# Start of a fused FFT and gated feed-forward kernel on one core: batch 0 loaded with a cast and folded by TensorE, its shuffle through DRAM in blocks, weights on the GpSimd queue

## The chip, the cores and the metric

The kernel runs on one core of a Trainium2 chip. The metric is the device time of one execution in microseconds. Three runs of the kernel before gave 648.35, 649.7 and 650.36 us (median 649.7). A further execution was profiled; its own time is given with the profile.

## The reference: what is computed

The input `x` has the shape (8, 3008, 256). A two-dimensional Fourier transform is taken over sequence and feature dimension, and its real part goes through a gated feed-forward layer: two projections, the first cut at zero, are multiplied and projected back:

```
X   = fft(fft(x, axis=1), axis=2).real            # (8, 3008, 256)
tok = X.reshape(24064, 256)
out = (max(tok @ w_gate, 0) * (tok @ w_val)) @ w_out   # w_gate, w_val: 256 x 1536, w_out: 1536 x 256
```

All inputs and the output are float32. The kernel computes products in bfloat16.

## The kernel before

**The transform.** 3008 is split as 94 x 32 (`NA`, `NB`). Since x is real, the transform has a mirror symmetry, and the kernel uses it twice: rows r and S - r are formed from the same two products (the "direct" and the "mirrored" half of each output block), and the input is *folded* first: row j is added to its mirror row, and columns d and 256 - d are added and subtracted. `fold` (line 96) does this for batches 1 to 7 on GpSimd, from four tiles (`xla`, `xlb` low half of the rows, `xha`, `xhb` mirrored rows), in 23 pieces per batch; the mirrored rows come by an indirect load (line 92) that walks the partitions backwards. Batch 0 has a path of its own: `load_first` (line 123) brings eight plain pieces on SP's queue, `fold_first` (line 131) folds columns only, on VectorE and GpSimd, and stage 1 adds the mirrored rows with a second set of tables, `w1h`.

**Stages of the transform.** `stage1` (line 170) multiplies by the 94-point tables (`w1`, and `wz` for the two end rows), two rows per call, and copies the result to the tile `t1`. `shuffle_out` (line 199) writes `t1` to a DRAM buffer `Td`, and `shuffle_in` (line 204) reads it back with partition and free index exchanged, as the tile `t4` with 12 slabs, four for each of the three blocks (`NBLK`) of a batch. `rotate` (line 210) repairs one column of `t4` by a small product. `stage2` (line 218) makes the 32-point transform of a block in two halves (`cs` 0 and 1), writes the block `pq`, and after half 1 sends row 0 of it through DRAM to get it on all partitions (`nb`, lines 236 and 237).

**The weights.** The transform over the feature dimension is multiplied into the weights. `load_w` loads three column groups n = 0, 1, 2 (called W0, W1, W2; `i` 0 is gate, 1 is value), `pair_w` (line 272) adds and subtracts their halves, `fold_w` (line 278) multiplies them with a cosine or sine table `cd` in float32 and writes `wc`, `ws`, and `wm` (scaled `ws`).

**The layer.** A step t is one batch, block and slice of 128 of the 1536 hidden columns: 8 x 3 x 12 = 288 steps. `gate` and `mirror_gate` make G (lines 517, 518, 524), `value` makes V (line 532), VectorE and ACT combine them, `mirror_h` (line 552) multiplies the mirrored half on GpSimd, except in the first block, where VectorE does it; `out_piece` (line 581) multiplies by `w_out`, and `store` (line 632) writes rows to DRAM. Steps 0 to 11 are the first block and run without the output products; from step 12 on two steps form a pair, and the output products of 12 steps earlier run between.

**What sets the order.** All engines run in the order of the program, written out by hand. The dictionary `extra`, filled by `at(t, ...)` (line 640 on), places transforms, weight folds and loads of later batches behind single steps; `plan` gives the steps of stage 1, shuffle, rotation and stage 2 for the next batch. `pace` hands GpSimd the pieces of `fold`, so many per step. A one-element copy to `seen` on GpSimd (line 457) waits for the shuffled batch 0; the indirect loads of batch 1, the load of `wo`, `pair_w` of W2 and the fold of batch 1 stand behind it on that engine. SP issues its transfers in program order too: x of batch 0, W0, half of W1, the shuffle, the rest of W1, W2, x of batch 1.

**At the end**, the last output block is copied out in four pieces (line 586); nothing is stored after the first, the first two together after the second, and the others by one, over SP's and ACT's queues.

**Warm products.** 32 products of a zero tile (`WARM`, line 338) run on TensorE ahead of all.

Of the kernel before, what the change touches and what calls it, by code (L numbers as in the profile page):

```python
# [19 lines left out]
WARM = 32  # L20
# [23 lines left out]
def kernel(ctx: ExitStack, tc, x, w_gate, w_val, w_out, out):  # L44
# [51 lines left out]
    def fold(b, eng):  # L96


        eo = xt[b]["eo"] = tp.tile([NA, J, D], BF16, tag="eo", name="eo")
        for half, chunks in enumerate(((1, 3, 5, 7), (9, 11, 13))):  # L100
# [16 lines left out]
            if 1 < b < B - 1:  # L117
                load_x(b + 1, half, nc.sync)


    FIRST = (0, 28, 4, 24, 8, 20, 12, 16)

    def load_first():
        t = {0: x_tile(True, 0), 1: x_tile(True, 1), 2: x_tile(False, 1), 3: x_tile(False, 0)}
        for r in FIRST:
            nc.sync.dma_start(out=t[r // JH][:, r % JH:r % JH + 4, :],
                              in_=view(x, r * D, [[NB * D, 96], [1, 4 * D]]))
        t["e"] = [tp.tile([NA, J, D], BF16, tag="eo", name="eo") for i in range(2)]
        xt[0] = t

    def fold_first(r, n, op, eng):

        t, e = xt[0][r // JH][0:NA], xt[0]["e"][r // 16]
        lo = r % 16

        def part(a, n, o, op, swap):
            p0 = free(t, (a % JH) * D + 1, [D, n], [1, H - 1])
            p1 = free(t, (a % JH) * D + D - 1, [D, n], [-1, H - 1])
            eng.tensor_tensor(e[:, a:a + n, o:o + H - 1], p1 if swap else p0, p0 if swap else p1, op=op)  # L139

        if op == ALU.add:
            part(lo, n, 1, ALU.add, False)
            eng.tensor_copy(free(e[:], lo * D, [D, n], [H, 2]), free(t, (lo % JH) * D, [D, n], [H, 2]))
        elif r == 16:
            part(0, 1, H + 1, ALU.subtract, False)
            part(1, n - 1, H + 1, ALU.subtract, True)
        else:
            part(lo, n, H + 1, ALU.subtract, r > 16)
# [12 lines left out]
    def early(name):  # L161

        if turn["v"] % 2 == 0:
            turn["t"] = psv.tile([128, 2, 512], F32, tag="v", name=name)
        turn["v"] += 1
        return turn["t"][:, (turn["v"] - 1) % 2, :]
# [3 lines left out]
    def stage1(b, c, evac):  # L170
        if b not in t1t:
            t1t[b] = tp.tile([96, 16, D], BF16, tag="t1", bufs=1, name="t1")
        t1 = t1t[b]
        eo, eh = xt[b]["e"] if b == 0 else (xt[b]["eo"], None)
        ps = early("ps1") if b == 0 else borrow("ps1")
        for i in range(2):
            jj = 2 * c + i
            o = ps[0:96, i * D:(i + 1) * D]
            if jj and b == 0:
                nc.tensor.matmul(o, lhsT=w1[:, jj, :], rhs=eo[:, jj, :], start=True, stop=False)  # L180
                nc.tensor.matmul(o, lhsT=w1h[:, NB // 2 - jj, :], rhs=eh[:, NB // 2 - jj, :], start=False, stop=True)  # L181
            elif jj:
                nc.tensor.matmul(o, lhsT=w1[:, jj, :], rhs=eo[:, jj, :], start=True, stop=True)  # L183
            else:
                ends = (eo[:, 0, :], eh[:, 0, :] if b == 0 else eo[:, J - 1, :])
                for cs, lo, hi in ((0, 0, H + 1), (1, H + 1, D)):
                    for k in range(2):
                        nc.tensor.matmul(ps[0:96, lo:hi], lhsT=wz[:, cs, k, :], rhs=ends[k][:, lo:hi],
                                         start=(k == 0), stop=(k == 1))
        dst = free(t1[:], 2 * c * D, [H, 4], [H // 2, 2], [1, H // 2])  # L190
# [5 lines left out]

    t4t = {}

    def shuffle_out(b, c0, c1):
# [103 lines left out]
    with tc.tile_pool(name="sp", bufs=1, space=SB) as sp:  # L303
# [159 lines left out]
        for _ in fold(1, pl):  # L463
            pass
# [291 lines left out]
```

## Time and profile before

| what | value |
|---|---|
| runs shown | 648.35, 649.7, 650.36 us |
| profiled execution, its own time | 646.91 us |
| its span, first to last instruction | 645.1 us |
| mean granted TensorE clock | 0.987 |
| busy share: TensorE, VectorE, ACT, GpSimd | 96%, 85%, 69%, 81% |
| start to the first gate product | 36.42 us |
| first block (steps 0 to 11) | 36.42 to 64.03 us |
| steps 12 to 287 | 64.03 to 627.42 us |
| output products of the last block | 627.42 to 637.93 us |
| from there to the end of the span | 7.17 us |

Rows of a timeline read: start, duration, engine, line, operation, output <- inputs, partitions x elements, count, and in brackets the idle time before with what ended it. PE is TensorE's product, PEld its weight load, DVE VectorE, POOL GpSimd, SPq, ACTq and POOLq the engines' issue of transfers. Product records overlap: the time one takes in a row of products is read from the distance of the starts.

### The profile page before, as it was taken

The page shows a single profiled execution, that of the slowest core. Times are in us where ns is not written, and L with a number is a line of the kernel's source. Part 1 is how long each engine was busy: PE and PEld are TensorE (multiplying, and loading weights), DVE is VectorE, ACT ScalarE, POOL GpSimd, SP SyncE. Part 2 cuts the span into 40 slices and gives each one's busy share as a digit, 9 for nine tenths or more (in the row PEclk, how much of TensorE's full clock was granted, in tenths as well). Part 3 has the DMA queues.
Part 4 walks back from the last instruction along what each step waited for, and adds up shares of the span by engine and source line. Part 5 has one row for each costly group of instructions (what it writes and reads, how often), then busy time and mean ns, then how long its engine had stood idle before and what let it go on. Part 6 is the DMA issues. An engine that isn't in the chain of part 4 may idle for free.

```text
span 645.1 us, 11866 instructions
## 1 busy us (share of the span) xinstructions
PE 618.7 (96%) x4231; PEld 410.4 (64%) x4231; DVE 549.3 (85%) x642; ACT 444.7 (69%) x846; POOL 521.9 (81%) x436
## 2 busy tenths in 40 slices
PE   6878999899999999999999999999999999999995
PEld 3423666666666666666666666676666666666664
DVE  9847888788988988988988897888988898899991
ACT  5455687667677767677777776777677777766660
POOL 9559989999999999999998999898555555556661
PEclk9699999999999999999999999999999999999999
DMA  9694753562735284344723555211512133212114
GB/s 248 197 242 68 173 147 83 153 161 67 207 83 137 43 234 103 106 102 114 195 65 87 121 142 150 59 33 37 156 51 60 46 93 93 67 33 65 32 39 92
DMA packets 35635, 70.72 MB, mean 110 GB/s; under 512 B 6124, under 2 KB 23508, under 8 KB 32244
## 3 DMA queue, kind: packets, MB, share of 16 engines
q1 hardware_dynamic: 32152, 57.92, 34.2%
q0 software_dynamic: 3120, 11.80, 8.0%
q8 instruction: 33, 0.54, 0.4%
q10 hardware_dynamic: 304, 0.25, 0.2%
q14 instruction: 26, 0.21, 0.1%
HBM read 39.77 MB, written 30.96 MB: 110 GB/s over the span
## 4 chain that ended last, share of the span: by engine, by line
PE 82%; DMA 5%; POOL 5%; DVE 3%; ACT 2%; issue 1%; SPq 1%; ACTq 0%; POOLq 0%; DVEq 0%
PE po L581 35%; PE V L532 17%; PE G L524 8%; PE G L518 8%; PE G L517 8%; DMA t<-Td 2%; DMA Td<-t 2%; PE ps L183 2%; POOL eo L139 2%; PE ps L225 1%; PE psw L282 1%; DVE E L539 1%; POOL h L552 1%; SPq L632 1%; DVE h L545 1%
## 5 line engine op out<-in xcount | busy, mean ns | idle before, releaser
L552 POOL TENSOR_TENSOR h<-gm,E 128x992 bf16<-128x992 f32 (+1 forms) x138 | 319.9, 2318 | 87.2 <-DVE E L559 51.7
L581 PE MATMUL po<-wo,h 128*128 128x256 bf16 (+2 forms) x2304 | 326.0, 272 | 0.0
L581 PEld LDWEIGHTS <-h 128*128 128x128 bf16 (+2 forms) x2304 | 231.7, 103 | 106.1
L526 ACT ACTIVATE gm<-G 128x496 f32<-128x496 f32 (+1 forms) x288 | 170.3, 591 | 101.0 <-PE G L524 95.9
L545 DVE TENSOR_TENSOR h<-gs,V 128x1024 bf16<-128x1024 f32 (+3 forms) x150 | 173.7, 1158 | 54.9 <-PE V L532 40.5
L539 DVE SCALAR_TENSOR_TENSOR E<-nb,af,V 128x496 f32<-128x496 bf16 (+1 forms) x276 | 190.2, 730 | 12.3 <-POOL h L552 5.6
L519 ACT ACTIVATE gs<-G 128x497 f32<-128x497 f32 (+2 forms) x288 | 169.7, 589 | 26.2 <-PE G L518 24.1
L559 DVE SCALAR_TENSOR_TENSOR E<-E,V 128x992 f32<-128x992 f32 (+1 forms) x138 | 164.3, 1190 | 0.0
L524 PE MATMUL G<-pq,wm 128*128 128x496 bf16 (+1 forms) x288 | 107.9, 375 | 2.3 <-ACT gs L519 2.2
L518 PE MATMUL G<-pq,ws 128*128 128x497 bf16 (+2 forms) x288 | 107.9, 375 | 0.6 <-DVE pq L232 0.6
L517 PE MATMUL G<-pq,wc 128*128 128x497 bf16 (+2 forms) x288 | 107.9, 375 | 0.0
L532 PE MATMUL V<-pq,ws 128*128 128x497 bf16 (+2 forms) x288 | 85.4, 374 | 3.5 <-DVE E L539 3.4
L532 PE MATMUL V<-pq,wc 128*128 128x497 bf16 (+2 forms) x288 | 85.5, 375 | 0.0
L594 ACT COPY os<-po 128x512 f32<-128x512 f32 x63 | 36.9, 586 | 17.6 <-PE po L581 17.0
L518 PEld LDWEIGHTS <-ws 128*128 128x128 bf16 x288 | 28.2, 98 | 32.6
L193 ACT CAST t<-ps 96x512 bf16<-96x512 f32 x63 | 36.6, 581 | 8.7 <-PE ps L181 6.7
L532 PEld LDWEIGHTS <-wc 128*128 128x128 bf16 x288 | 27.7, 98 | 22.5 <-issue 3.9
L517 PEld LDWEIGHTS <-wc 128*128 128x128 bf16 x288 | 28.2, 98 | 20.3 <-issue 2.9
L110 POOL TENSOR_TENSOR eo<-xla 94x254 bf16<-94x254 f32 x56 | 39.9, 722 | 1.0
L107 POOL TENSOR_TENSOR xla<-xla,xha 94x510 f32<-94x510 f32 x28 | 35.4, 1264 | 2.2
L110 POOL TENSOR_TENSOR eo<-xlb 94x254 bf16<-94x254 f32 (+1 forms) x42 | 33.7, 813 | 0.7
L532 PEld LDWEIGHTS <-ws 128*128 128x128 bf16 x288 | 26.5, 97 | 9.7 <-issue 6.3
(125 smaller groups left out, 380.9 us busy)
## 6 DMA issues: line engine op xcount, KB each, us to landing
out_dram<-os SPq DMA_DIRECT2D x126, 128.0 KB
out_dram<-os SPq DMA_DIRECT2D x86, 64.0 KB
Td<-t SPq DMA_DIRECT2D x7, 768.0 KB
t<-Td SPq DMA_DIRECT2D x7, 768.0 KB
xla<-in_x_dram SPq DMA_DIRECT2D x7, 720.0 KB
xlb<-in_x_dram SPq DMA_DIRECT2D x7, 640.0 KB
nb<-Nd SPq DMA_DIRECT2D x24, 128.0 KB
out_dram<-os SPq DMA_DIRECT2D x39, 48.0 KB
```

What stands on the lines that cost most here:

```text
L110: yield eng.tensor_tensor(e1[:, :, o:o + H - 1], x1[:, :, 1:H], free(x1, D - 1, [D, n], [-1, H - 1]), op=op)
L517: nc.tensor.matmul(G[:, ds], lhsT=wc[0][:, fs], rhs=pq[:, 0, ds], start=True, stop=False)
L518: nc.tensor.matmul(G[:, ds], lhsT=ws[0][:, fs], rhs=pq[:, 1, ds], start=False, stop=True)
L519: nc.scalar.activation(pair(t, "gs")[:, t % 2, ds], G[:, ds], ACTF.Relu)
L524: nc.tensor.matmul(G[:, cols], lhsT=wm[0][:, f * 128:(f + 1) * 128], rhs=pqt[b, blk][:, 1, cols], start=False, stop=True, skip_group_check ...
L526: nc.scalar.activation(pair(t, "gm")[:, t % 2, cols], G[:, cols], ACTF.Relu)
L532: nc.tensor.matmul(pair(t, "V")[:, t % 2, cs], lhsT=w[:, f * 128:(f + 1) * 128], rhs=pqt[b, blk][:, min(k, 1), cs], start=(k == 0), stop=( ...
L539: nc.vector.scalar_tensor_tensor(pair(t, "E")[:, t % 2, cols], nbt[b, blk][:, cols], af[:, f:f + 1], pair(t, "V")[:, t % 2, cols], op0=ALU ...
L545: nc.vector.tensor_tensor(pair(t, "h")[:, k, 0, 0:ds.stop - ds.start], pair(t, "gs")[:, k, ds], pair(t, "V")[:, k, ds], op=ALU.mult)
L552: eng.tensor_tensor(free(pair(t, "h")[:], 1024 * (t % 2) + 512 + w - 1, [1024, n], [-1, w]), pair(t, "gm")[:, k, cols], val[:, k, cols], o ...
L559: nc.vector.scalar_tensor_tensor(E[:, :, cols], E[:, :, cols], 2.0, V[:, :, cols], op0=ALU.mult, op1=ALU.subtract)
L581: nc.tensor.matmul(po[0:m, i, :], lhsT=pair(t - f + ff, "h")[:, ff % 2, sg, g * 128:g * 128 + m], rhs=wo[:, ff, :], start=(ff == 0), stop= ...
```

## The change

- **Batch 0's load** goes from eight plain loads on SP's queue to six on GpSimd's, which write bfloat16 from float32. The upper rows come by indirect loads in mirrored partition order.
- **Its fold** falls away as work of VectorE and GpSimd. `first_products` lets TensorE read the loaded rows forwards and backwards and accumulate, with the table `w1`, a negated copy `n1` made by VectorE, and a third pair of `wz` tables. Upper and lower rows of a group of chunks go in separate passes; the copies go out in the groups 1 to 3, 4 and 5, 6 and 7, 0, the last on ACT's queue.
- **The shuffle back** is two transfers, block 0 and the other two blocks. `rotate` works on a range; `seen` waits for block 0 only.
- **W0 and W1** are loaded on GpSimd's queue behind x; W2 stays on SP behind the shuffle. Only W0 is folded ahead of the first block; W1 at steps 0 to 3, W2 at 4 to 7, the other four halves of `stage2` at 5, 8, 9 and 10.
- **Small tables** are made earlier and partly on other engines; a bit mask takes the place of the float residue for the 32-point table; `wm` is made by VectorE from `ws`.
- **Later batches**: loads of x at fixed steps, stage 1 of batch 1 from step 12 instead of 18, one common plan for the others, 15 pieces of batch 1's fold before the loop, the rest and all others at a slower pace, 23 pieces per 36 steps from step 56.
- **The end**: each of the four last pieces is stored at once, the last over three queues, and the direct half of the last block by GpSimd's queue.
- **Warm products** are 16 at the start, 2 and 6 later.

```diff
-WARM = 32
+WARM = 16
...
+    def load_first(r, n):
+        name = "lo" if r < NB // 2 else "hi"
...
+        dst = xt[0][name][:, r % 16:r % 16 + n, :]
+        if r < NB // 2:
+            nc.gpsimd.dma_start(out=dst, in_=view(x, r * D, [[NB * D, 96], [1, n * D]]))
         else:
+            k = {(24, 8): 0, (20, 4): 1, (16, 4): 2}[r, n]
+            nc.gpsimd.indirect_dma_start(
+                out=dst.rearrange("p j d -> p (j d)"), out_offset=None,
+                in_=view(x, 0, [[n * D, NB // n * NA], [1, n * D]]),
+                in_offset=bass.IndirectOffsetOnAxis(ap=ixf[:, k:k + 1], axis=0))
...
+    def first_products(c, upper):
+        if not upper:
+            psf[c] = early("ps1")
+        for i in range(2):
+            jj = 2 * c + i
+            o = psf[c][0:96, i * D:(i + 1) * D]
+            v = xt[0]["hi"][0:NA, 0 if jj == 0 else NB // 2 - jj, :] if upper else xt[0]["lo"][0:NA, jj, :]
+            back = free(v, D - 1, [-1, H - 1])
...
+            for k, (lo, hi, w, rhs) in enumerate(((0, H + 1, ce, v[:, 0:H + 1]), (1, H, ce, back),
+                                                  (H + 1, D, up, v[:, 1:H]), (H + 1, D, dn, back))):
+                nc.tensor.matmul(o[:, lo:hi], lhsT=w, rhs=rhs, start=not (upper or i or k),
+                                 stop=upper and i == 1 and k == 3, skip_group_check=True)
...
-        if cs == 1:
+        if cs == 1 and (b or blk):
...
-            nc.scalar.activation(wm[i][:, sl_], ps[:], ACTF.Copy, scale=s2[:])
+            nc.vector.tensor_scalar(wm[i][:, sl_], ws[i][:, sl_], scalar1=s2[:], scalar2=None, op0=ALU.mult)
...
-    load_w(0)
-    load_w(1, (0,))
...
+        warm(WARM)
+        load_first(0, 8)
...
+        load_first(24, 8)
+        pl.iota(pi[:], pattern=[[0, 1]], base=0, channel_multiplier=1)
+        load_first(8, 4)
+        load_first(20, 4)
+        load_first(12, 4)
+        load_first(16, 4)
...
+        load_w(0, pl, (0,))
...
+        load_w(0, pl, (1,))
+        load_w(1, pl)
...
+        def negate(a, b_):
+            dve.tensor_scalar(n1[:, a:b_, :], w1[:, a:b_, :], scalar1=-1.0, scalar2=None, op0=ALU.mult)
...
+        angles(0, 9)
+        table(1, 9)
...
+        negate(1, 9)
+        group((1, 2, 3), False)
+        angles(9, J)
+        table(9, 16)
+        group((1, 2, 3), True)
...
+        evacuate(0, 3, psf[3], "act")
+        shuffle_out(0, 1, 4)
+        negate(9, 16)
...
+        group((4, 5), False)
+        group((4, 5), True)
...
+        shuffle_out(0, 4, 6)
...
+        group((6, 7, 0), False)
+        warm(2)
+        group((6, 7, 0), True)
+        evacuate(0, 6, psf[6], "act")
+        evacuate(0, 7, psf[7], "dve")
+        evacuate(0, 0, psf[0], "act")
+        shuffle_out(0, 6, 8)
+        shuffle_out(0, 0, 1, nc.scalar)
...
+        shuffle_in(0, 0, 4)
+        shuffle_in(0, 4, NKA)
+        load_w(2, nc.sync)
...
+        warm(6)
+        pair_w(0, 0, dve)
...
+        pair_w(0, 1, dve)
+        fold_w(0, 0, 0, "act")
+        fold_w(0, 0, 1, "dve")
+        fold_w(0, 1, 0, "act")
+        fold_w(0, 1, 1, "dve")
+        pair_w(1, 0, dve)
+        rotate(0, 0, 4, dve.tensor_copy)
+        stage2(0, 0, 0, "act")
+        stage2(0, 0, 1, "dve")
+        pair_w(1, 1, dve)
...
-        pl.tensor_copy(seen[:, 0:1], t4t[0][0:1, NKA - 1, 0:1])
+        pl.tensor_copy(seen[:, 0:1], t4t[0][0:1, 3, 0:1])
         for half in range(2):
             load_x(1, half, nc.sync)
         pl.dma_start(out=wo[:], in_=view(w_out, 0, [[D, 128], [128 * D, NF], [1, D]]))
...
+        pair_w(2, 0, pl)
+        first = fold(1, pl)
+        for k in range(15):
+            next(first)
...
-                if g:
-                    store(b, blk, sg, os_, 0 if g == 1 else g, g + 1, (nc.sync, nc.scalar))
+                store(b, blk, sg, os_, g, g + 1, (nc.sync, nc.scalar) if g < 3 else (nc.sync, nc.scalar, nc.gpsimd))
...
-                store(b, blk, sg, os_, 0, 4, (nc.sync,))
+                store(b, blk, sg, os_, 0, 4, (nc.gpsimd if t - f == len(steps) - NF else nc.sync,))
...
+    at(3, pair_w, 2, 1, nc.vector, (0,))
+    at(4, pair_w, 2, 1, nc.vector, (1,))
+    at(4, rotate, 0, 4, NKA)
     for k in range(4):
-        at(3 + k, fold_w, 2, k // 2, k % 2, "dve" if k % 2 else "act")
-        at(8 + k, stage2, 0, 1 + k // 2, k % 2, "dve")
-    at(9, nyquist)
+        at(k, fold_w, 1, k // 2, k % 2)
+        at(4 + k, fold_w, 2, k // 2, k % 2)
+    for t, blk, cs, e in ((5, 1, 1, "dve"), (8, 2, 1, "act"), (9, 1, 0, "dve"), (10, 2, 0, "act")):
+        at(t, stage2, 0, blk, cs, e)
+    at(11, nyquist)
...
+    plan = {0: (12, 13, 14, 16, 18, 20, 21, 22), 1: (4, 5, 7, 10, 14, 17, 19, 20)}
...
+        at(t0 + (21 if b else 22), shuffle_out, b + 1, 0, 8)
+        at(t0 + (21 if b else 22), shuffle_in, b + 1, 0, NKA)
+        at(t0 + 28, rotate, b + 1)
+        for i, k in enumerate((28, 29, 31, 34, 35, 37)):
             at(t0 + k, stage2, b + 1, i // 2, i % 2, "act")
+        if b < B - 2:
+            for half, k in enumerate((5, 24) if b else (13, 22)):
+                at(t0 + k, load_x, b + 2, half, nc.sync)
...
-        paced["due"] += 0 if t < 22 else 1 if t < 46 else 0.85 if t < 100 else 0.7
+        paced["due"] += 0 if t < 12 else 1 if t < 20 else 0.72 if t < 56 else 23 / 36
```

More of the change, by code (lines that the diff above doesn't have):

```diff
@@ L376, with warm @@
-        for r in FIRST[4:]:
-            fold_first(r, 4, ALU.add, dve)
-        for r in FIRST[:-2]:
-            fold_first(r, 4, ALU.subtract, pl)
-        for r in FIRST[-2:]:
-            fold_first(r, 4, ALU.subtract, dve)
-        pi = sp.tile([128, 1], I32, tag="pi")
-        pl.iota(pi[:], pattern=[[0, 1]], base=0, channel_multiplier=1)
+        psk = psg.tile([128, 512], F32, tag="g", name="psk")
+        def warm(n):
+            for k in range(n):
+                nc.tensor.matmul(psk[:], lhsT=wk[:, 512:640], rhs=wk[:, 0:512], start=True, stop=True)
@@ L460 @@
         pl.dma_start(out=wo[:], in_=view(w_out, 0, [[D, 128], [128 * D, NF], [1, D]]))
-        for i in range(2):
-            pair_w(2, i, pl)
-        for _ in fold(1, pl):
-            pass
+        pair_w(2, 0, pl)
+        first = fold(1, pl)
+        for k in range(15):
+            next(first)
     nc.vector.memset(one[:], 1.0)
-    stage2(0, 0, 0, "act")
-    rotate(0)
-    fold_w(1, 1, 0, "act")
-    stage2(0, 0, 1, "dve")
     gp = ctx.enter_context(tc.tile_pool(name="gp", bufs=2, space=SB))
```

266 lines of the change are left out of this document (113 added, 153 removed).

## The prediction

> **What bounds the kernel now.** I first read busy time in stretches cut where the stages change. Columns: stretch, then busy us and count of PE, PEld, DVE, ACT, POOL, then clock, DMA share and GB/s.
>
> ```profile
> 0.00:36.42 36.42, 26.17 (x103) 12.98 (x104) 29.52 (x53) 18.45 (x35) 28.14 (x44) 0.81 0.81 235
> 36.42:64.03 27.61, 23.61 (x125) 8.85 (x123) 18.98 (x32) 15.93 (x30) 20.18 (x28) 1.00 0.69 130
> 200.00:300.00 100.00, 98.45 (x684) 66.28 (x683) 88.13 (x98) 72.87 (x140) 97.85 (x86) 1.00 0.44 117
> 300.00:400.00 100.00, 98.55 (x698) 67.08 (x697) 87.41 (x98) 72.54 (x140) 92.85 (x78) 1.00 0.50 125
> 500.00:627.42 127.42, 127.42 (x882) 86.03 (x880) 116.06 (x130) 89.08 (x171) 74.87 (x33) 1.00 0.23 59
> 637.93:645.10 7.17, 0.00 (x0) 0.00 (x0) 0.42 (x1) 0.00 (x0) 0.00 (x0) 0.80 0.31 69
> ```
>
> From 64 us on, TensorE sets the time; what can be won lies in 36.42 us before the first gate product, 27.61 us of first block, a few stalls, and 7.17 us behind the last product. The chain of waits says what fills the start, and the timeline gives the places on it:
>
> ```profile
> 7.93 10.42 POOL eo L139 x6
> 24.59 0.30 SPq L201
> 25.41 2.76 DMA wst<-in_moe_w_val_dram
> 28.95 4.39 PE psw L282 x16
> ```
> ```profile
> 26.40 1.48 SPq L207 DMA_DIRECT2D t<-Td  x3
> 32.26 0.32 POOL L457 COPY seen<-t 1x1 bf16<-1x1 bf16 x1 [4.78 <-DMA t<-Td]
> 35.06 0.18 PE L213 MATMUL ps<-t,rot 128*128 128x12 bf16 x1 [1.41 <-ACT pq L230]
> 36.42 0.37 PE L517 MATMUL G<-pq,wc 128*128 128x496 bf16 x1
> 37.37 0.37 PE L518 MATMUL G<-pq,ws 128*128 128x496 bf16 x1 [0.57 <-DVE pq L232]
> ```
>
> Six GpSimd folds carry the chain to 18.35; the last shuffle piece goes out at 24.59; W1's second half lands 28.2; the transformed batch is in at 32.26; the first gate product starts 36.42. So the start is folding, then shuffle and weight folding side by side.
>
> **The change, part by part.** *x of batch 0.* Six software-queue loads that cast replace eight plain ones. No row shows a casting load. The plain ones:
>
> ```profile
> 4.00:16.00 12.00, 7.65 (x37) 3.84 (x35) 11.50 (x13) 7.27 (x14) 11.75 (x12) 0.93 1.03 276
> L92 POOL DMA_INDIRECT xhb<-in_x_dram,ix x6 | 5.6, 935 | 1.0 <-issue 0.6
> 35.58 1.13 POOL L460 DMA_DIRECT2D wo<-in_moe_w_out_dram  x1
> xha<-in_x_dram,ix POOLq DMA_INDIRECT x7, 8.9
> ```
>
> 96 x 32 KB is 3.15 MB; at 276 GB/s 11.4 us. The first issue ends about 1.8 (GpSimd starts 0.85, 0.94 an issue), 1.8 us pass from a shuffle issue to the next transfer that waits for it (24.59 to 26.40): 15.0, and one more for the iotas between issues: x is in at 16. Bounds: written bytes set the pace (5.7 us), but six issues and iotas end near 8.5 and the last piece needs 3: 11.5. Above: 752 KB in 8.9 us, a rate seen beside other traffic: 4.2 such pieces, 37 us, 39 in all. I take the plain rate, since those 8.9 us hold three loads at once.
>
> *Stage 1.* The folds (10.42 us of GpSimd, and VectorE's share) go; TensorE takes the mirrored reads: 128 products of some 127 columns instead of 30 of 256 and four half ones. Price from the spacing of the starts:
>
> ```profile
> 15.08 0.42 PE L181 MATMUL ps<-eo,w1h 94*96 94x256 bf16 x1
> 15.30 0.42 PE L180 MATMUL ps<-eo,w 94*96 94x256 bf16 x1
> 57.34 0.39 PE L225 MATMUL ps<-m,t 128*128 128x128 bf16 x4
> 57.57 0.37 PE L524 MATMUL G<-pq,wm 128*128 128x496 bf16 x1
> ```
>
> 0.22 per 256 columns at the start's low clock, so 0.11 for 127; 0.06 at full clock. All but the last group (24 products: chunks 6, 7, 0 against the last load) lie under the load. Those cost 2.6 us (1.4 at full clock), the copy 0.27 + 0.58: the last shuffle piece is ready at 19.5, and at 1.8 more it is written, 21.3.
>
> *Shuffle and weights.* Now only the first 256 KB of three such pieces gates what follows, but W0 and W1 (2.1 MB) run on the other queue behind x. Bounds: 1.8 us (the shuffle row) and 5.9 (26.40 to 32.26, three pieces and weights); I take 3.5: 24.8. The weight side: W0 is in at 16 + 3.8 = 19.8; four fold_w groups follow six warm products.
>
> ```profile
> 23.87 4.05 PE L282 MATMUL psw<-wst,cd 128*64 128x512 f32 x8
> 44.93 1.08 PE L282 MATMUL psw<-wst,cd 128*64 128x512 f32 x4
> 45.94 0.38 PE L524 MATMUL G<-pq,wm 128*128 128x496 bf16 x1
> ```
>
> A group takes 1.0 at full clock, 2.0 at half. From 21.2 (18.6 and six warm products of 0.43) mixed clock makes 26.0. Rotation, two transforms and their copies add 2.0 (35.06 to 37.37 before, less 1.0 of a weight group between, and the copy on VectorE): the first gate product at 28.0, between 26.5 (shuffle alone) and 29.5 (half clock throughout). **Gain 8.4.**
>
> Moved past queues: eight weight loads become GpSimd issues, about 8 x 1.1 us, all before that engine's wait for the shuffle; SP loses them and its x loads, so shuffle-out finds it empty. The index columns move to VectorE (seven small ones, 0.15 to 0.3 each), under the x load. `seen` waits for one piece; behind it stand x of batch 1, wo, pair_w and the batch 1 fold, all some 6 us earlier than at 32.26.
>
> *First block.* Eight fold_w groups instead of five stand in it: 3 x 1.0 more; the second rotation 0.2. The scaled copy moves from ACT to VectorE, from SBUF; what ACT held up:
>
> ```profile
> L524 PE MATMUL G<-pq,wm 128*128 128x496 bf16 x12 | 4.5, 375 | 2.3 <-ACT gs L519 2.2
> ```
>
> 3.2 - 2.2 is 1.0; some of the 4.0 us TensorE idles here will take weight groups too, so 0.5. **Loss 0.5**, between a gain of 1 and a loss of 3.2.
>
> *Steady loop.* Waits of TensorE from 64.03 to 627.42, what GpSimd does in it, the ends of its fold of batch 1, and a transfer on the chain:
>
> ```profile
> PE V L532 <- DVE E L539: 3.4, 5, 1.8
> PE psr L213 <- DMA t<-Td: 1.4, 1, 1.4
> L552 POOL TENSOR_TENSOR h<-gm,E 128x992 bf16<-128x992 f32 (+1 forms) x137 | 317.6, 2319 | 86.9 <-DVE E L559 51.5 <-ACT gs L519 29.2 <-ACT t L214 3.0
> 48.41 0.22 POOL L105 TENSOR_TENSOR eo<-xla,xha 94x4 bf16<-94x4 f32 x1 [6.49 <-PE psw L282]
> 71.58 0.86 POOL L115 TENSOR_TENSOR eo<-xlb 94x127 bf16<-94x127 f32 x2
> 112.44 4.29 DMA nb<-Nd
> ```
>
> The 1.8 is batch 1's late second transform (its row nb lands at 116.7), which the new plan starts four to five steps earlier; the rest falls where GpSimd is 98% busy. A step lasts 563.4 / 276 = 2.04 us; GpSimd needs 1.16 of it for h, and 24 us a batch for 23 fold pieces (48.41 to 72.44): at 0.85 pieces a step 2.05, full; at 23/36 it is 1.83. So the 3.4 go, the 1.4 may stay (shuffle to rotation is seven steps as before). **Gain 3.0**, from -1 to 3.4.
>
> *End.*
>
> ```profile
> 632.96 0.38 ACT L592 COPY os<-po 113x256 f32<-113x256 f32 x1
> 637.93 0.42 DVE L586 COPY os<-po 112x256 f32<-112x256 f32 x1 [0.89 <-PE po L581]
> 639.10 4.02 SPq L632 DMA_DIRECT2D out_dram<-os  x9
> SPq L632 <- DMA out_dram<-os: 2.9, 2, 2.4
> ```
>
> SP issues until 643.1, the end comes 2.0 later. The six stores of the block's direct half move to GpSimd, 633.3 + 6 x 0.94 = 639.0, its last own part 639.9, landed 641.9. SP has 11 parts of 0.45 in groups of three per 1.3 us and is through near 639.3, or 642.2 if the 2.9 of waits stay. **Gain 2.2**, from 0 to 3.2.
>
> Sum: 8.4 - 0.5 + 3.0 + 2.2 = 13.1. The profiled execution took 646.9 (span 645.1 and 1.8 around it): 633.8. The median shown, 649.7, stands 2.8 above it, so the time to be measured is **636.6**; 26.5 or 29.5 for the start and the other bounds put its own range at 632 to 643.
>
> **Rivals.** *Batch 1 is late on GpSimd (17%).* Stage 1 of batch 1 now begins at step 12, not 18, and it was late already. If x still arrives at 48.4, four h products (9.3) in its way end it at 81.7; chunk 7 needs it at step 21, 28.0 + 28.1 + 9 x 2.04 = 74.4: TensorE stalls 7.3. 643.9. For it: 6 MB share the engines with the shuffle (0.8 of its own, 1.5 of W1 and W2, 3.0 of x, 0.8 of wo). Against: x is asked for 6 us sooner.
>
> *GpSimd and VectorE block each other (10%).* In the trace a GpSimd sum stretches a VectorE scalar operation:
>
> ```profile
> 24.88 1.26 POOL L275 TENSOR_TENSOR wst<-wst 128x512 f32<-128x512 f32 x1
> 24.95 1.27 DVE L38 TENSOR_SCALAR q<-q 128x128 f32<-128x128 f32 x1
> 30.18 0.23 DVE L38 TENSOR_SCALAR q<-q 128x128 f32<-128x128 f32 x1
> ```
>
> 1.04 more. Some 28 scalar operations and casts stand on VectorE ahead of its last copy, while GpSimd issues 14 loads. If half are hit, 14.6 us; VectorE, with some 11 of the 17 us until then taken by the old rows' lengths, has 6 to spare: 8 later, 644.6. No row has such an operation beside an issue. The Trainium skill, page "SBUF — State Buffer", section "Who interferes with whom", says that VectorE in a two-port mode and GpSimd exclude each other for a whole instruction, the writing of software descriptors included. By that rule this rival is what happens; the trace agrees for sums (1.27 against 0.23) and is silent for issues.
>
> *Casting loads are slow (10%; the other side).* At the 8.9 us row x is in at 39, 23 later, all on the path: 636.6 + 23 = 659.6, slower. It decides from 16 + 13.1 = 29 us of arrival on, that is below 125 GB/s. For it: the only software rows of this size. Against: those rows share the engines.
>
> *The start doesn't get shorter (5%).* Weights behind x share the engines with the shuffle, so the gate product stays near 36 and the block costs its 3.2; with the loop's and end's share lost to it as well, 649.
>
> **How the numbers follow.** Forecast 58%, at 636.6. About 0.3% (2 us) is what a measurement can tell from no change. Faster: 58 + 17 + 10 = 85%, of which I keep 83, since two rivals together reach 652; same 6%, slower 11%. Range 631.5 to 647: below, nearly all bounds at their best; above, the first two rivals with 2.5 to spare; left out are the slow loads, the last rival and a little at the lower end, some 18%.
>
> **What would show it.** Right: the last first-batch copy near 19.5, the first gate product at 27 to 29, first block 27 to 31 us, no E wait near 117 and about 100 of 100 busy between 200 and 400, under 6 us from the last copy to the end. Wrong: x landing after 20; TensorE waiting on eo at stage 1 of batch 1; VectorE scalar operations of 1 us beside issues; the span's end set by a GpSimd store.

## The result, and the profile after

The changed kernel took 634.44 us (median of 633.5 to 635.41, four executions), the kernel before beside it 649.16 us. The ratio is 0.9772, with a 95% interval of 0.9749 to 0.9795: faster by about 14.7 us. Measured again in two later groups of runs, the same two kernels were 11.7 and 12.8 us apart. The profiled execution took 635.41 us (span 633.6, mean granted clock 0.995), 11.5 us less than the profiled one before.

Busy time in stretches of the changed kernel, cut at the same events as before (columns as before: PE, PEld, DVE, ACT, POOL with counts, clock, DMA share, GB/s):

```profile
0.00:25.70 25.70, 20.22 (x178) 12.25 (x179) 18.93 (x55) 11.14 (x24) 15.76 (x41) 1.00 0.79 204
25.70:54.77 29.07, 27.82 (x134) 9.47 (x134) 20.02 (x36) 17.53 (x35) 20.12 (x27) 0.94 0.88 192
54.77:616.28 561.51, 557.98 (x3913) 379.94 (x3913) 496.16 (x553) 408.06 (x779) 470.33 (x366) 1.00 0.38 101
616.28:626.80 10.52, 10.48 (x97) 9.44 (x94) 3.03 (x5) 2.14 (x5) 6.99 (x8) 1.00 0.44 106
626.80:633.60 6.80, 0.00 (x0) 0.00 (x0) 0.42 (x1) 0.00 (x0) 0.51 (x1) 0.77 0.24 66
```

| stage | before, us | after, us | gain | predicted gain |
|---|---|---|---|---|
| start to the first gate product | 36.42 | 25.70 | 10.72 | 8.4 |
| first block | 27.61 | 29.07 | -1.46 | -0.5 |
| steps 12 to 287 | 563.39 | 561.51 | 1.88 | 3.0 |
| last output products and the end | 17.68 | 17.32 | 0.36 | 2.2 |
| span | 645.1 | 633.6 | 11.5 | 13.1 |

More came from the start than predicted, less from each of the other three. The clock column shows two things: the start now runs at 1.00 where it had 0.81 (read from 5.9 us on: before that the trace has no clock record, and the column stands at 1.00 for want of one), and the first block has 0.94 where it had 1.00.

The chain of waits through the start of the changed kernel:

```profile
10.57 0.43 ACT w L313
11.04 3.31 PE ps L197 x52
14.36 0.43 PE psk L351 x2
14.79 1.36 PE ps L197 x24
16.17 0.59 ACT t L174
16.79 5.03 DMA Td<-t
21.90 2.67 DMA t<-Td
25.48 0.70 DVE pq L235
```

Before, six GpSimd folds stood here until 18.35. Now the chain runs over VectorE and ACT, which make the tables, until the table `w` is ready at 11.00; the load of x isn't on it. TensorE runs stage 1 without a pause from 11.04, the last piece is copied at 16.76, and the shuffle takes over: 5.03 us to write `Td`, 2.67 to read the first block back. The timeline of TensorE behind it:

```profile
17.36 4.15 PE L285 MATMUL psw<-wst,cd 128*64 128x512 f32 x16
24.61 0.17 PE L216 MATMUL psr<-t,rot 128*128 128x4 bf16 x1 [3.10 <-DMA t<-Td]
...
25.70 0.37 PE L552 MATMUL G<-pq,wc 128*128 128x496 bf16 x1 [0.25 <-ACT pq L233]
...
27.44 1.98 PE L285 MATMUL psw<-wst,cd 128*64 128x512 f32 x4
...
30.91 1.08 PE L285 MATMUL psw<-wst,cd 128*64 128x512 f32 x4
```

All four folds of W0 are done at 21.51, then TensorE waits 3.10 us for the shuffle. The first fold of W1 at 27.44 takes 1.98, the next 1.08: after the wait TensorE runs at half speed for a while. The DMA traffic in the first 12 us, in stretches:

```profile
0.00:4.00 4.00, 2.69 (x7) 1.03 (x8) 1.76 (x7) 1.49 (x2) 2.53 (x11) 1.00 0.35 41
4.00:8.00 4.00, 4.00 (x26) 1.99 (x24) 3.25 (x15) 1.77 (x3) 3.38 (x6) 1.00 0.98 167
8.00:12.00 4.00, 3.21 (x54) 2.92 (x52) 3.79 (x12) 2.63 (x7) 3.99 (x12) 1.00 1.07 182
```

The last column counts written bytes, as far as this shows: (41 + 167 + 182) GB/s x 4 us is 1.56 MB, and x of batch 0 is 1.57 MB in bfloat16, 3.15 MB in float32. Some of the 1.56 MB are W0's, whose first transfer goes out at 8.90. The landing of the pieces is a closer measure; the three of the upper rows:

```profile
hi<-in_x_dram,ixf POOLq DMA_INDIRECT x3, 5.6
```

5.6 us is the median from issue to landing. The last of them was issued at 7.32 and landed 5.7 us later, at 13.0. So x was in at 13.0, not 16, and TensorE didn't wait for it: its last group began at 14.79, straight behind the one before. The waits of TensorE in the steady loop, and then the stores of the end, on the timelines of GpSimd and SP (E is the tile that VectorE makes of V for `mirror_h`; h, the product of gate and value, is what `out_piece` reads):

```profile
PE ps L228 <- ACT t L217: 2.2, 7, 0.3
PE psr L216 <- DMA t<-Td: 1.3, 1, 1.3
```
```profile
622.50 3.02 POOL L666 DMA_DIRECT2D out_dram<-os  x6 [2.02 <-ACT os L626]
```
```profile
623.38 7.99 SPq L666 DMA_DIRECT2D out_dram<-os  x11
```

The waits for E (3.4 us before) are gone. In their place stand seven waits of 0.3 us for the copy of the rotated column. At the end GpSimd is done with its six stores at 625.52, while SP issues its 11 parts until 631.37, 2.2 before the end of the span. The 7.99 us of this row is the longest of its kind: in the eight other profiles with the same end the 11 parts take 6.7 to 7.3 us.

### The profile page after: what moved, and what is told of

The parts are those of the page before. It is cut to its first block, busy times and chain, and to the rows that moved or that the text cites. A ratio compares the mean times of both kernels' runs of the same rounds, so it can differ in the third digit from the quotient of the medians.

```text
span 633.6 us, 12015 instructions
## 1 busy us (share of the span) xinstructions
PE 616.5 (97%) x4318; PEld 411.1 (65%) x4318; DVE 538.6 (85%) x647; ACT 438.9 (69%) x841; POOL 513.7 (81%) x440
## 4 chain that ended last, share of the span: by engine, by line
PE 92%; DMA 3%; ACT 1%; DVE 1%; issue 1%; POOL 1%; POOLq 0%; SPq 0%; DVEq 0%
PE po L616 38%; PE V L567 19%; PE G L559 9%; PE G L553 9%; PE G L552 9%; PE ps L228 2%; PE ps L159 2%; DMA t<-Td 2%; DMA Td<-t 1%; PE psw L285 1%; PE ps L197 1%; POOL out_dram L666 0%; DVE h L580 0%; ACT t L217 0%; PE ps L163 0%
## 5 line engine op out<-in xcount | busy, mean ns | idle before, releaser
L553 PEld LDWEIGHTS <-ws 128*128 128x128 bf16 x288 | 28.2, 98 | 33.1 <-issue 0.6
L174 ACT CAST t<-ps 96x512 bf16<-96x512 f32 x60 | 34.9, 582 | 4.7 <-PE ps L197 1.9
L559 PEld LDWEIGHTS <-wm 128*128 128x128 bf16 x288 | 28.1, 98 | 9.0 <-issue 6.5
```

The costliest lines, as they stand in the source:

```text
L553: nc.tensor.matmul(G[:, ds], lhsT=ws[0][:, fs], rhs=pq[:, 1, ds], start=False, stop=True)
L559: nc.tensor.matmul(G[:, cols], lhsT=wm[0][:, f * 128:(f + 1) * 128], rhs=pqt[b, blk][:, 1, cols], start=False, stop=True, skip_group_check ...
```

## The experiments

Each stands beside executions of the kernel before on the same chip; the gain is taken from their median there. The four runs e4 to e7 have no run of the unedited changed kernel beside them; they are set against c0_same and f1_same by their gains.

| run | median, us | before, us | gain | ratio, 95% interval |
|---|---|---|---|---|
| c0_same | 636.13 | 647.81 | 11.7 | 0.9800 to 0.9831 |
| e1_old_end | 636.62 | 647.81 | 11.2 | 0.9813 to 0.9855 |
| e2_old_plan | 640.44 | 647.81 | 7.4 | 0.9863 to 0.9897 |
| e3_no_warm | 641.60 | 647.81 | 6.2 | 0.9898 to 0.9930 |
| e4_w1_after | 637.13 | 648.10 | 11.0 | 0.9817 to 0.9853 |
| e5_warm_gap | 635.45 | 648.10 | 12.7 | 0.9763 to 0.9802 |
| e6_plain_x | 640.27 | 648.10 | 7.8 | 0.9847 to 0.9919 |
| e7_w1_after_end | 636.18 | 648.10 | 11.9 | 0.9800 to 0.9844 |
| f1_same | 635.62 | 648.44 | 12.8 | 0.9779 to 0.9820 |
| f2_gap_and_end | 632.47 | 648.44 | 16.0 | 0.9739 to 0.9793 |
| f3_seen_all | 635.71 | 648.44 | 12.7 | 0.9785 to 0.9814 |
| f4_gap_end_rotate | 631.87 | 647.73 | 15.9 | 0.9726 to 0.9770 |

**The changed kernel itself.** c0_same and f1_same have no edit; they are the control of their groups.

> The changed kernel once more, unaltered, as the measure for the runs beside it. Theory: 634.4 us again, first gate product at 25.7, span's last 6.8 us behind the last output product. If the pause of 1.8 us that SP and ACT both show at 627.7 in the first profile was a single event, this profile ends 1.5 to 2 us sooner behind the last product; if it belongs to the kernel, it stands there again.

> The changed kernel once more, beside the two below: 635.5 to 636.5 us, 11.5 to 14 below the kernel before.

Their executions run from 633.7 to 636.7 us, so a difference below about 1 us isn't told apart by such medians. Part of this spread lies outside the span: 1.8 to 2.9 us in c0_same. What makes up a larger spread comes up with the last two runs. Of the two readings that c0_same was to tell apart, neither holds whole: from the last output product to the end its profile takes 6.0 us instead of 6.8.

**The new end, taken back.**

```diff
-                store(b, blk, sg, os_, g, g + 1, (nc.sync, nc.scalar) if g < 3 else (nc.sync, nc.scalar, nc.gpsimd))
+                if g:
+                    store(b, blk, sg, os_, 0 if g == 1 else g, g + 1, (nc.sync, nc.scalar))
...
-                store(b, blk, sg, os_, 0, 4, (nc.gpsimd if t - f == len(steps) - NF else nc.sync,))
+                store(b, blk, sg, os_, 0, 4, (nc.sync,))
```

> Changed kernel with the stores of the last block as before (direct half on SP, first two pieces together, SP and ACT only). Theory A, the trace: the new end is worth 0.4 us (17.7 against 17.3 from the last block's output products on), so this run is 0 to 0.5 us slower than the changed kernel. Theory B, the prediction: 2.2 us slower, if the pause at 627.7 was a single event.

636.62 against 636.13: 0.5 us, less than the spread. By the profiles the last output products and what is behind them took 17.9 us here and 16.5 in c0_same, where the same code had needed 17.3 in the first profile of the changed kernel. By the medians the new end is worth 0.5 us, by these two profiles 1.4, not 2.2.

**The old plan for later batches.** The steps of stage 1, shuffle, rotation and stage 2, the places of the loads and the pace of the folds are those of before; the start is the new one.

```diff
-    plan = {0: (12, 13, 14, 16, 18, 20, 21, 22), 1: (4, 5, 7, 10, 14, 17, 19, 20)}
+    plan = {0: ((18, 19, 20, 21, 22, 23, 24, 25), 26, 32, (33, 34, 35, 37, 39, 41)),
+            1: ((10, 11, 13, 14, 16, 17, 19, 20), 21, 28, (29, 31, 32, 34, 35, 37)),
+            2: ((4, 5, 7, 10, 11, 13, 16, 17), 18, 25, (26, 28, 29, 31, 34, 35))}
...
-        paced["due"] += 0 if t < 12 else 1 if t < 20 else 0.72 if t < 56 else 23 / 36
+        paced["due"] += 0 if t < 22 else 1 if t < 46 else 0.85 if t < 100 else 0.7
```

> Changed kernel with the plan, the pace of the fold, the places of the loads of x and the whole fold of batch 1 ahead of the loop as before; start, first block and end are new. Theory A, the trace: the loop part is worth 1.9 us (561.5 against 563.4), so 636.3. Theory B, the prediction: 3.0, so 637.4, with TensorE's waits on E back at 3.4 us in total. Rival: the waits came from the late start of batch 1 alone, which is gone with the new start: 634.4, no E wait above 1 us.

4.3 us slower than c0_same, more than either theory gave. The waits of TensorE from 54 us on:

```profile
PE psr L218 <- DMA t<-Td: 3.8, 1, 3.8
PE V L568 <- DVE E L575: 3.7, 5, 1.9
```

The E waits are back with nearly their old sum, 3.7 against 3.4: the new plan, with its loads and its pace, is what removes them. The wait for a shuffle is 3.8 us; it stands at 383.8 us and is batch 5's, as the 1.4 us of the kernel before is, and behind it the granted clock stands at half from 384.9 to 388.4. So the plan is worth more beside the new start than the 1.88 us that the table shows for the loop: it pays for itself and for what the earlier start would otherwise have lost.

**No warm products.** None at the start, and not the two and six later.

```diff
-WARM = 16
+WARM = 0
...
-        warm(2)
...
-        warm(6)
```

> Changed kernel without any warm product (16, 2 and 6 left out). Theory A, the clock carries the start: stage 1 runs at 0.11 us for 127 columns instead of 0.056, 128 products take 14 us instead of 7.2, the last shuffle piece is ready 4 us or more later, the first gate product at 29 to 30, 638 to 639 us. Rival: stage 1 is dense enough to raise the clock by itself within some 3.5 us; only its first 30 products are slow: 1 to 2 us later, 635.5 to 636.5.

5.5 us slower. A row of its chain of waits:

```profile
6.91 14.02 PE ps L197 x128
```

128 products in 14.02 us, 0.11 each, back to back; the changed kernel starts them 0.056 apart. The first gate product comes at 30.38 instead of 25.70. That is still 6 us earlier than in the kernel before, but 4.7 of the 10.7 us gained at the start hang on the warm products, and stage 1's own products didn't bring TensorE to the higher rate in 14 us. The granted-clock column reads 1.00 in this whole stretch, but the trace has no clock record before 25.7 us, so here the product rate is the evidence and the column isn't.

**W1 behind the shuffle.** W1's four transfers go on SP's queue behind the first block of the shuffle; its pairing and folds follow one step later. e7_w1_after_end has the same and stores the first two pieces of the end together.

```diff
-        load_w(1, pl)
...
         shuffle_in(0, 0, 4)
+        load_w(1, nc.sync)
...
-        pair_w(1, 0, dve)
         rotate(0, 0, 4, dve.tensor_copy)
         stage2(0, 0, 0, "act")
         stage2(0, 0, 1, "dve")
+        pair_w(1, 0, dve)
...
-        at(k, fold_w, 1, k // 2, k % 2)
+        at(min(k + 1, 3), fold_w, 1, k // 2, k % 2)
```

> Changed kernel with W1 loaded on SP's queue behind the first part of the shuffle back (not on GpSimd's behind x), its halves paired behind the first two transforms and folded at steps 1, 2, 3, 3. Theory A, W0 and W1 hold up the shuffle on the DMA engines: the last write of the shuffle takes 2.0 to 2.5 us instead of 5.03, block 0 is back at about 21.5, the first gate product at 22.8 to 23.2 (bounded by the weight folds), 3 us sooner, and the run 3 us faster than the changed kernel, some 633. Rival: the write of 5.03 is the price of the last write itself; it stays near 5 and nothing is won, or W1's late arrival stalls step 1 and takes it back.

> The kernel with W1 behind the shuffle, and with a mixed end: direct half on GpSimd and three queues for the last piece as in the changed kernel, the first two pieces stored together as before (16 issues on SP and ACT instead of 22). Theory A: the end is bound by issues and their waits on SP and ACT; 6 issues less end it 1.5 to 2 us sooner: 16.5 us from the last output products becomes 14.5 to 15, 631 us in all. Rival: the end is bound by the landing of the last stores: same as without it.

The chain of waits of e4_w1_after:

```profile
16.77 2.24 DMA Td<-t
...
23.77 14.87 DMA wst<-in_moe_w_val_dram
```

With 1 MB of weights out of its way the write of `Td` takes 2.24 us instead of 5.03, and the first gate product comes at 23.62, 2.1 earlier. But TensorE now waits 4.6 us for h in the first block: 1.7 at 27.8, behind the sums that pair W1, which this run has VectorE do after the transforms, and 2.1 at 40.9, behind W2's value half, which lands at 38.6 and holds up VectorE for 4.4. Step 12 starts its value product at 56.29, in the changed kernel at 54.98. So 2.8 of the 5.03 us are the price of W1 on the same DMA engines (W0 was still ahead of the shuffle in this run); moving the bytes only moves the wait. e7_w1_after_end gave 636.18, no better than the changed kernel, where 631 was expected. Its end took 16.1 us from the last output products, as long as that of e4_w1_after with three more parts on SP; 14.5 to 15 had been expected.

**Warm products in the wait.** 13 products of the zero tile in the 3.1 us in which TensorE waits for the shuffle.

```diff
+        pk = psg.tile([128, 512], F32, tag="g", name="psk2")
+        for k in range(13):
+            nc.tensor.matmul(pk[:], lhsT=wk[:, 512:640], rhs=wk[:, 0:512], start=True, stop=True)
         pair_w(1, 0, dve)
```

> Changed kernel with 13 more warm products between the folds of W0 and the rotation, where TensorE waits 3.1 us for the shuffle. Theory A: the wait lets the clock fall; the first products of the block and the first weight group (1.98 us instead of 1.08) run slow for it; filled, the first block takes 1.0 to 1.3 us less, 635. Rival: the block's length has other causes (VectorE, weights): no change within 0.5 us, the weight group stays at 2.0.

The first fold of W1 takes 1.01 us instead of 1.91, and step 12 starts at 54.09 instead of 54.98, though the shuffle was 0.5 later in this profile: from the first gate product on the block is 1.35 us shorter. Its median is the lowest of its group, but its executions lie between 632.51 and 636.79. The profiled one is the 636.79; TensorE waits 2.43 us in it for the shuffle of batch 1, until 90.97, and the granted clock stands at half from 92.4 to 95.8.

**Plain loads of batch 0.** The same six transfers from the same queue, but float32 to float32. Stage 1 of batch 0 reads a zero tile of bfloat16 once each piece has landed, so batch 0's transform is left out; stage 1 has the same products, and six of one element beside them.

```diff
+            t.update({0: x_tile(True, 0), 1: x_tile(True, 1), 2: x_tile(False, 1), 3: x_tile(False, 0)})
...
-            v = xt[0]["hi"][0:NA, 0 if jj == 0 else NB // 2 - jj, :] if upper else xt[0]["lo"][0:NA, jj, :]
+            v = wk[0:NA, 0:D]
```

> Changed kernel with the six loads of batch 0 on the same queue in the same order but without the cast, into the float32 tiles of x; stage 1 runs the same products on a tile of zeros, each group behind one product that reads an element of its load. Batch 0's part of the output is left out this way. Theory A, the cast shortens the load because half the bytes are written: plain loads run at 276 GB/s as before, the last lands at 15.5 to 16.5 instead of about 12.5, the first gate product comes 1.5 to 3 us later (637.5 to 639). Rival: the load's pace is that of the bytes read, cast or not: within 0.5 us of the changed kernel.

640.27 us, where 637.5 to 639 was expected. Two rows of its chain, and from the list of its transfers the median landing of the last two upper pieces:

```profile
3.14 7.04 DMA xha<-in_x_dram,ixf
...
19.59 2.73 PE ps L205 x24
```
```profile
xhb<-in_x_dram,ixf POOLq DMA_INDIRECT x2, 8.1
```

The last group starts at 19.59 instead of 14.79 and takes 2.73 us instead of 1.36. The plain upper pieces land 7.0 to 8.6 us after their issue, the casting ones 5.2 to 5.7; the last, issued at 7.30, lands at 15.9 instead of 13.0. So casting is not slower than plain loading but quicker, by 2.9 us for the whole of x. The 4.8 us by which the last group starts later are no measure of that, since its load had landed 3.5 us before it: TensorE waited 1.4 us for the first upper piece, until 10.2, and the granted clock then stood at half from 12.8 to 23.0.

**GpSimd waits for the whole shuffle.**

```diff
-        pl.tensor_copy(seen[:, 0:1], t4t[0][0:1, 3, 0:1])
+        pl.tensor_copy(seen[:, 0:1], t4t[0][0:1, NKA - 1, 0:1])
```

> GpSimd waits for all blocks of the shuffle, not for block 0 alone, so x of batch 1, wo and the fold of batch 1 start some 3 us later. If the fold of batch 1 is just in time (its last piece was done at 72.5 in the changed kernel, and stage 1 wants it at step 21, some 73 to 75), TensorE now waits for eo at stage 1 of batch 1 for 0 to 3 us: 636 to 639. If batch 1 has slack, no wait and the same time; if it is already late (the rival of 17%), all 3 us and more.

635.71 against 635.62: the same. The delay was 1.3 to 1.7 us rather than 3 (`seen` at 26.30 instead of 24.63 to 24.97), the fold of batch 1 began at 41.84 instead of 39.28 to 40.36, and TensorE still didn't wait for eo. Batch 1 has at least that much slack. In this profile the granted clock stands at half for 6.8 us around the first gate product, 23.9 to 30.7.

**Two edits, then a third.** f2_gap_and_end joins the warm products in the wait with an end that stores the first two pieces together and keeps three queues for the last. f4_gap_end_rotate adds the rotation of batch 1 two steps later.

```diff
-                store(b, blk, sg, os_, g, g + 1, (nc.sync, nc.scalar) if g < 3 else (nc.sync, nc.scalar, nc.gpsimd))
+                if g:
+                    store(b, blk, sg, os_, 0 if g == 1 else g, g + 1, (nc.sync, nc.scalar) if g < 3 else (nc.sync, nc.scalar, nc.gpsimd))
...
-        at(t0 + 28, rotate, b + 1)
-        for i, k in enumerate((28, 29, 31, 34, 35, 37)):
+        at(t0 + (28 if b else 30), rotate, b + 1)
+        for i, k in enumerate((28, 29, 31, 34, 35, 37) if b else (30, 31, 32, 34, 35, 37)):
```

> Two edits together: 13 more warm products while TensorE waits for the first block of the shuffle, and the first two pieces of the end stored together with the last one on three queues. If the clock's fall in the wait costs the first weight group 1 us and the end's stores queue behind each other, 1 to 2 us below the changed kernel (634 to 635). If both are noise, within 0.7 us of it.

f2_gap_and_end has a median of 632.47, but its five executions are 632.21, 632.46 and 632.47 at a mean clock of 0.998 to 1.0, and 635.21 and 636.39 at 0.995 and 0.996. The profiled one is the 635.21; the three near 632 have no profile. Its timeline has one long wait in the loop:

```profile
90.59 0.19 PE L216 MATMUL psr<-t,rot 128*128 128x12 bf16 x1 [2.11 <-DMA t<-Td]
```

First the stretches of the changed kernel around the first gate product, then those of f2_gap_and_end around that wait (the clock is the third number from the end):

```profile
24.00:26.00 2.00, 1.11 (x10) 0.61 (x10) 0.69 (x2) 0.59 (x1) 0.78 (x2) 1.00 1.03 305
26.00:28.00 2.00, 1.84 (x6) 0.54 (x6) 1.85 (x5) 0.58 (x1) 1.69 (x3) 0.59 1.03 374
28.00:30.00 2.00, 2.00 (x7) 0.28 (x4) 0.29 (x1) 0.54 (x2) 2.00 (x2) 0.55 1.19 353
30.00:32.00 2.00, 2.00 (x10) 0.55 (x9) 1.25 (x2) 1.03 (x3) 1.41 (x2) 1.00 0.98 217
```
```profile
88.00:92.00 4.00, 1.59 (x15) 1.01 (x13) 2.26 (x3) 1.30 (x3) 3.92 (x5) 0.98 0.91 235
92.00:96.00 4.00, 4.00 (x20) 2.34 (x19) 0.71 (x1) 2.09 (x5) 2.46 (x2) 0.59 0.05 19
```

The rows are mixtures of 1.00 and 0.50: the first fence holds (0.41 + 0.45) x 2 / 0.5 = 3.4 us of half clock, the second (0.02 + 0.41) x 4 / 0.5, the same. It begins 1.8 us after the wait of 3.10 us has ended and 1.25 after the one of 2.11, and costs 1.7 us beside the wait (3.4 us of work at half speed). The first block of f2_gap_and_end, whose wait is filled, has 1.00 throughout.

The other profiles bear this out. From 20 us to the last product, all ten waits of TensorE of 2.4 to 3.8 us have a half clock of 3.4 us beside them (6.8 in f3_seen_all), which begins between 0.8 us before the end of the wait and 2.1 us after it. Of five waits of 2.0 to 2.3 us two have one (2.11 in f2_gap_and_end, 2.05 in e3_no_warm) and three have none; of fourteen of 0.9 to 1.9 us none has. No half clock begins there without such a wait.

The Trainium skill describes this on the page "TensorE: Matmul & The Clock Gate" (section "What's actually happening"): a clock gate goes by windows of about 3.4 us that run freely and don't begin anew with the kernel; an idle one halves the clock, a busy one restores it. The lengths agree: 3.4 us, 6.8 in f3_seen_all, 10.2 in e6_plain_x and 13.7 in the start of the kernel before, all multiples of one length. That a window has to be idle throughout isn't borne out, since waits of 2.05 to 3.15 us were enough. Windows that run freely would explain why waits of one length do it in one case and not in another; whether the three executions of f2_gap_and_end near 632 had the same wait isn't shown. If the half clock behind this wait makes the spread, taking the wait away should take the spread away:

> The two edits of the run with gap and end, and the rotation of batch 1 two steps later (its transforms at steps 30, 31, 32, 34, 35, 37). In that run TensorE waited 2.1 us for the shuffle of batch 1 at 88.5, and the granted clock then stood at 0.50 from about 92 to 95.5 us; its executions fell into two groups, 632.2 to 632.5 at a clock of 0.998 to 1.0 and 635.2 to 636.4 at 0.995. Theory: the wait starts the clock's fall, and the fall makes the group. Then the wait goes, the clock reads 1.00 from start to end, and all executions lie near 631 to 633. If the two groups come from something else, the spread of 632 to 636 stays.

631.87 us, and the five executions lie between 631.28 and 632.12. The same stretches in its profile:

```profile
88.00:92.00 4.00, 4.00 (x29) 2.67 (x28) 3.75 (x6) 2.65 (x5) 3.92 (x5) 1.00 0.98 240
92.00:96.00 4.00, 3.68 (x33) 2.66 (x31) 2.78 (x4) 2.93 (x7) 4.00 (x3) 1.00 0.58 153
```

The wait for the shuffle is 0.4 us, the clock stays at 1.00 up to the last product, and the spread of 4 us has become one of 0.8. That fits the theory and doesn't prove it: in f2_gap_and_end two of five executions took over 635 us, and at that rate five in a row stay below by chance in 8% of cases. This kernel beats the change as it was, 15.9 us below the kernel before against 11.7 to 14.7; f2_gap_and_end's median lies as far below it, 16.0, but two of its executions lie near 636. On its timeline SP issues 8 parts at the end instead of 11:

```profile
622.34 4.94 SPq L670 DMA_DIRECT2D out_dram<-os  x8
```

4.94 us instead of 7.99 from the first to the last, and the last output products and the end took 15.6 us (613.99 to 629.6) instead of 17.3. Against the eight other profiles with 11 parts (16.1 to 16.8) that is 0.5 to 1.2 us less, as in f2_gap_and_end (15.6 too); e7_w1_after_end has 16.1 with the same 8 parts, so what the fewer parts are worth isn't settled.

## Why the prediction was right or wrong

The direction and the range held: 636.6 was forecast between 631.5 and 647, 634.44 came. The sum of the terms was 13.1 against 11.5 in the profiles, and two terms were off by about 2 in opposite directions: the start by 2.3 too little, the end by 1.8 too much; block and loop lacked about 1 each. That the total came near is in part luck. The rest is the step from the profiled execution to the median: I added 2.8 us because the profiled run of before lay that far below the median shown; that of after lay 1.0 above its own. A single execution's distance from the median doesn't carry over. Of the signs named ahead, the block of 29.07 us, the loop without E wait and busy near 100 between 200 and 400 came; the last copy (16.8 instead of 19.5) and the first gate product (25.70 instead of 27 to 29) came earlier, and the end took 6.4 us from the last copy instead of under 6.

**Start, 8.4 forecast, 10.72 measured.** The term that failed is the weight side, "W0 is in at 16 + 3.8 = 19.8 ... mixed clock makes 26.0": the folds ran from 17.36 to 21.51 at full clock. Three of its inputs were off. x was in at 13.0 us, nearer the lower bound (11.5) than the plain rate that I chose; with plain loads, e6_plain_x, that rate's 16 came true (15.9). Then, the last group didn't wait for x, as I had it, but only for TensorE's own work and the tables ahead of it. And I priced stage 1 at the old start's 0.11 us a product; the warm products held it at 0.056, as e3_no_warm shows by their absence. The shuffle path came out right as a sum, by luck: the last piece was ready at 16.8, not 19.5, and the read took 2.67, not 3.5, but the write took 5.03 us, not 1.8, of which e4_w1_after puts 2.8 down to W1. It landed at 24.57; forecast 24.8. The first gate product at 25.70 lies below the 26.5 that I gave as the bound of the shuffle alone, because rotation and transforms took 1.1, not 2.0. Three of my sums were slips: 24.8 + 2.0 is 26.8, not 26.5; four folds at half clock from 21.2 with 2.0 behind them end at 31.2, not 29.5; and 752 KB, taken in units of 1024 bytes, go 4.1 times into 3.15 MB, not 4.2. None of them entered the forecast.

**First block, -0.5 forecast, -1.46 measured.** The step that failed took the block at full clock. The wait for the shuffle is what the faster weight side leaves, and behind it TensorE runs 3.4 us of the block at half clock, 1.7 us lost by that reckoning: more than the whole excess of 0.96. e5_warm_gap takes the half clock away, and the block is 1.35 us shorter.

**Loop, 3.0 forecast, 1.88 measured.** "So the 3.4 go, the 1.4 may stay" came true in its first half. In the second only the number did, by luck: the 1.4 us was the shuffle of batch 5 and went, and 1.3 us came for that of batch 1. First the kernel before, then the changed one:

```profile
390.35 0.18 PE L213 MATMUL psr<-t,rot 128*128 128x12 bf16 x1 [1.45 <-DMA t<-Td]
```
```profile
90.75 0.19 PE L216 MATMUL psr<-t,rot 128*128 128x12 bf16 x1 [1.32 <-DMA t<-Td]
```

What the step left out is that rotation and first transform now share a step (28 and 28), so TensorE waits 0.3 us for the copy between them in each of seven batches: 2.2 us. 3.4 + 0.1 - 2.2 is 1.3. The waits for h fell by 0.2 (0.5 before, 0.3 after), and TensorE's busy time in the loop by 0.4 (558.42 before, 557.98 after); why it did stays open. The stretches between 200 and 400 us of the changed kernel show TensorE 99.4 to 99.7 of 100 busy, where it was 98.5:

```profile
200.00:300.00 100.00, 99.68 (x699) 68.03 (x697) 88.73 (x100) 73.27 (x140) 90.99 (x75) 1.00 0.38 102
300.00:400.00 100.00, 99.36 (x707) 67.74 (x706) 88.11 (x99) 73.52 (x141) 89.66 (x75) 1.00 0.45 119
```

**End, 2.2 forecast, 0.36 measured** (0.8 to 1.8 by the eight other profiles with this end, 16.1 to 16.8 us, against 17.7 and 17.9 with the old one; 0.5 by the median of e1_old_end). GpSimd's part was over-priced, 0.5 us an issue instead of 0.94. The step that failed is the 11 parts of SP: I had 639.3, or 642.2 if the waits stay. They stay. 11 parts took 7.99 us, with 1.9 of waiting for earlier stores, and 6.7 to 7.3 in the other profiles.

**The rivals.** Batch 1 late on GpSimd (17%): its fold began at 39.28, not 48.4, TensorE never waited for eo, and f3_seen_all shows slack beyond that. GpSimd and VectorE blocking each other (10%): the timeline of the changed kernel has VectorE's scalar operations inside GpSimd's issues of indirect loads:

```profile
3.12 1.39 POOL L129 DMA_INDIRECT hi<-in_x_dram,ixf  x1 [0.20 <-POOL ki L323]
...
3.59 0.38 DVE L308 TENSOR_SCALAR tq<-tt 94x432 f32<-94x432 f32 x1
4.01 0.38 DVE L309 TENSOR_SCALAR tq<-tq 94x432 f32<-94x432 f32 x1
...
7.75 0.36 DVE L308 TENSOR_SCALAR tq<-tt 94x384 f32<-94x384 f32 x1
8.14 0.57 DVE L309 TENSOR_SCALAR tq<-tq 94x384 f32<-94x384 f32 x1
```

Both of 432 columns took 0.38 us within an issue that lasted 1.39. Of the two of 384 columns, the second took 0.2 more, far from the 1.04 that the rival needed, and no scalar operation of VectorE ahead of its last copy took longer than 0.57. By the rule of the Trainium skill's page "SBUF — State Buffer", section "Who interferes with whom", that the prediction weighed, these would have waited out the issue, if they ran in a two-port mode; the trace doesn't show it. Slow casting loads (10%): excluded by the arrival at 13.0 us and by e6_plain_x. The start not getting shorter (5%): wrong as a whole, but its mechanism, weights sharing the engines with the shuffle, is real: W1 costs the write of `Td` about 2.8 us.

## What to carry to other kernels

Look at where TensorE waits 2 us or more, not only at how long: beside every wait of 2.4 us or more, and some of 2.0 to 2.3, the granted clock stood at half for about 3.4 us here, which cost another 1.7 us and probably made the executions spread by 4; a few products of a zero tile in the wait removed the half clock, and a consumer moved by two steps removed the wait with it. Price a stage that moves by the clock it will run at, not by the one it ran at. And when a load is moved out of the way of a transfer, name the next load behind it: here 2.1 us won at the first product were gone by step 12.

## What the runs showed that I had not expected

Loads that cast were quicker than plain ones: 3.15 MB of float32 were in 11.8 us after the first issue, with plain loads 14.6. Stage 1's products, 94 rows by 96 columns with 127 to 129 moving columns, ran 14 us back to back at 0.11 us each without getting faster, while the granted-clock column read 1.00. And at the end SP's queue lost 2.9 us to waits for earlier stores with 9 parts on it, 1.5 to 2.4 with 11, and 0.8 to 1.6 with 8.
